# Inverse roots and small scalings as operations of their own in a fused attention and two-MoE kernel

## The chip, the cores and the metric

The kernel runs on one core of a Trainium2 chip. The metric is device time in microseconds (us) of one execution; the number that stands for a kernel is the median of its runs.

## The reference, cut to what matters

```python
def _attn_ref(q, k, v, g_q, g_k):            # batch 4, 12 heads, 448 tokens, 64 channels
    def rmsnorm(x, g):
        rms = np.sqrt(np.mean(x * x, axis=-1, keepdims=True) + 1e-06)
        return x / rms * g
    scores = np.matmul(rmsnorm(q, g_q), rmsnorm(k, g_k).transpose(0, 1, 3, 2)) / np.sqrt(64)
    scores = scores - np.max(scores, axis=-1, keepdims=True)
    attn = np.exp(scores)
    attn = attn / (np.sum(attn, axis=-1, keepdims=True) + 1e-09)
    return np.matmul(attn, v)

h = x @ w_in                                  # x is 1792 x 768, w_in 768 x 2048
g = h * (1.0 / (1.0 + np.exp(-1.702 * h)))    # first layer
x = g @ w_out                                 # w_out 2048 x 768
h = x @ w_in2                                 # second layer, same sizes
out = (h * np.clip(h + 3.0, 0.0, 6.0) / 6.0) @ w_out2
```

Attention, a first MLP layer and a second one follow each other. The weights of both layers arrive as 64-bit floats and are decoded on the chip.

## The kernel before

Every product of fp32 accuracy is made from two fp16 pieces (a high and a low one), so each layer matmul is three fp16 matmuls. The work is cut into four batches of 448 tokens. A batch goes through these stages:

- **Norm.** `sums_of` loads two heads of q and k, squares them (ACT or GpSimd) and sums the squares (VectorE, L974). `root` turns 14 or 28 columns of sums into inverse roots: nine small VectorE instructions, L1003 to L1018. `put` multiplies (L1028), splits into pieces (L1034, L1046, L1049) and transposes by DMA.
- **Units** (`add_units`), 24 groups of one or two tiles of 128 queries a batch. A group is: scores on PE into one of two `s` buffers (L1203, L1206), the row maximum on VectorE (L1211), a scaling of the maximum on ACT (L1215), the exponentials with their sums on ACT (L1216), which free the `s` buffer, a scaling of the sums on ACT (L1221), a reciprocal on VectorE (L1224). In batch 0 the probabilities are then turned by PE with a diagonal that holds 1/sum (L1265) and copied out (L1275 on ACT, L1276 on VectorE). In batches 1 to 3 they are split into pieces and turned by DMA. A product with v (L1164, in batch 0 L1131) ends each pair of heads; its result is split by ACT (L1297) and VectorE (L1302) into `xt`.
- **First layer.** `add_in1` is 16 blocks of 18 matmuls (L1410), each followed by a gate on ACT (L1455) and a product and a split on VectorE (L1459, L494). `add_out1` is 6 blocks of 48 matmuls (L1478), each followed by an evacuation on ACT (L1494). Beside the first layer of batch b stands the attention of batch b + 1. The first layer of batch b + 1 begins when the last out-block of batch b is on its way.
- **Second layer** (L1654 and L1769), over two halves of the tokens, after all batches.

Beside batch 0 the first weight W1 is decoded, beside batch 1 the second, W2 (L613, L617, L634, L494 and others).

What runs where and in which order is decided while the program is built. Each operation is entered with the engines that may take it and a cost in ns for each (`ways`), and a list scheduler (`Plan.order`) places all of them, by rank and by numbers in `CFG`: `own` and `off` shift the rank of single operations or of whole stages, `bias` charges an engine for an operation that others may take. The five engines then execute their queues strictly in order; an instruction that waits holds up all behind it on its engine. Where the plan leaves PE without work for some time it inserts filler matmuls (L1959).

## Time and profile before

| | |
|---|---|
| median of 3 runs | 1146.96 us (1146.66 to 1147.59) |
| the profiled execution | 1147.63 us |
| its span, first to last instruction | 1145.8 us |
| PE, VectorE, ACT, GpSimd busy | 1065.3, 822.5, 721.3, 365.1 us |
| mean granted clock of PE | 0.985 of full speed |

A share of busy time is a mean over stages with different limits. Which engine bounds a stage is read from the busy times of that stage and from what PE waits for in it.

### The profile page before, as it was taken

The numbers are of one execution on the slowest core, as the hardware profiler recorded it, in microseconds if no ns is written. First come the engines' busy times: TensorE is split into PE (matmuls) and PEld (weight loads), VectorE is DVE, ScalarE is ACT, GpSimd is POOL, SyncE is SP. The second block draws the span as 40 slices with busy tenths as digits, with TensorE's granted clock in tenths as the row PEclk, the third lists the DMA queues.
The fourth block names the chain that finished last, engine by engine and source line by source line (L and its number), as shares of the span: only waits on it lengthen the run. The fifth ranks groups of instructions, "written<-read, shape, count | busy, mean of one in ns | idle before, by whom it ended". The sixth has DMA issues, their size and how long they took to land. (4 is left out here: it accounts for less than half of the span.)

```text
span 1145.8 us, 18018 instructions
## 1 busy us (share of the span) xinstructions
PE 1065.3 (93%) x6571; PEld 588.7 (51%) x6571; DVE 822.5 (72%) x1445; ACT 721.3 (63%) x1505; POOL 365.1 (32%) x335
## 2 busy tenths in 40 slices
PE   3888964999999999999999999999999999999998
PEld 1566531554554555545555555555555555555555
DVE  7998889998699764797756878594577455935342
ACT  5999758999868996578885646463565132512210
POOL 6764555353156201350001255552132103200000
PEclk9999985999999999999999999999999999999999
DMA  8977578999976997569895327633451151222033
GB/s 239 193 199 192 167 203 212 204 191 222 241 227 187 173 176 155 181 194 166 171 185 154 120 78 264 231 108 120 146 189 55 56 169 40 71 72 98 1 90 104
DMA packets 236712, 178.88 MB, mean 156 GB/s; under 512 B 194896, under 2 KB 220496, under 8 KB 235088
## 3 DMA queue, kind: packets, MB, share of 16 engines
q1 hardware_dynamic: 236624, 177.74, 59.4%
q8 instruction: 51, 0.84, 0.3%
q14 instruction: 37, 0.30, 0.1%
HBM read 97.88 MB, written 34.41 MB: 115 GB/s over the span
## 5 line engine op out<-in xcount | busy, mean ns | idle before, releaser
L1410 PE MATMUL mm<-xt,wa 128*128 128x448 f16 x1152 | 229.5, 357 | 7.0 <-DVE st L1459 6.8
L1478 PE MATMUL mm<-gt,wb 128*128 128x448 f16 x1152 | 226.7, 352 | 0.7 <-DVE wb L494 0.5
L1769 PEld LDWEIGHTS <-gt 128*128 128x128 f16 x1344 | 131.4, 98 | 92.3 <-issue 4.8
L1410 PEld LDWEIGHTS <-wa 128*128 128x128 f16 x1152 | 113.9, 100 | 114.3 <-issue 14.5
L1478 PEld LDWEIGHTS <-wb 128*128 128x128 f16 x1152 | 111.8, 99 | 103.9 <-issue 1.1
L1654 PEld LDWEIGHTS <-xt 128*128 128x128 f16 x1008 | 98.6, 98 | 93.7 <-issue 3.8
L1216 ACT ACTIVATE p<-s,smalls 128x448 f32<-128x448 f32 x168 | 120.7, 720 | 7.5 <-DVE p L494 3.4
L1654 PE MATMUL s<-wa,xt 128*128 128x448 f16 x576 | 114.1, 352 | 2.1 <-DVE st L1669 2.1
L1211 DVE TENSOR_REDUCE smalls<-s 128x2 f32<-128x896 f32 (+1 forms) x96 | 91.5, 963 | 4.1 <-PE s L1206 3.9
L494 DVE SCALAR_TENSOR_TENSOR p<-p,smalls 128x448 f16<-128x448 f32 x108 | 78.1, 752 | 22.4 <-ACT p L479 22.1
L1203 PE MATMUL s<-gt 128*128 128x448 f16 (+1 forms) x192 | 62.2, 370 | 30.2 <-ACT p L1216 28.3
L1654 PE MATMUL mm<-wa,xt 128*128 128x448 f16 x432 | 86.9, 352 | 0.9 <-ACT wb L1676 0.9
L479 ACT ACTIVATE p<-p,smalls 128x448 f16<-128x448 f32 (+2 forms) x120 | 75.8, 666 | 11.7 <-DMA xt<-p 8.6
L1769 PE MATMUL mm<-p,gt 128*128 128x384 f16 x384 | 72.0, 326 | 0.0
L1769 PE MATMUL mm<-gt 128*128 128x384 f16 x372 | 68.2, 326 | 0.0
L1206 PE MATMUL s<-gt 128*128 128x448 f16 (+1 forms) x192 | 61.9, 366 | 0.0
L1769 PE MATMUL s<-p,gt 128*128 128x384 f16 x288 | 56.1, 326 | 2.4 <-ACT wb L1805 1.2
L1769 PE MATMUL s<-gt 128*128 128x384 f16 x300 | 55.9, 326 | 1.0 <-DVE st L1669 0.6
L494 DVE SCALAR_TENSOR_TENSOR gt<-st,smalls,gt 128x448 f16<-128x448 f32 x64 | 52.4, 829 | 6.1 <-ACT gt L479 4.9
L1808 DVE SCALAR_TENSOR_TENSOR wb<-mm,smalls,wb 128x384 f32<-128x384 f32 x47 | 27.0, 611 | 41.0 <-PE mm L1769 41.0
L479 ACT ACTIVATE gt<-st,smalls 128x448 f16<-128x448 f32 x49 | 32.1, 661 | 29.9 <-DVE st L1459 26.2
L1265 PE MATMUL mm<-gt,p 128*128 128x128 f32 x336 | 44.1, 280 | 6.3 <-DVE xt L1276 1.9
(216 smaller groups left out, 1827.4 us busy)
## 6 DMA issues: line engine op xcount, KB each, us to landing
wr<-in_moe_w_in_dram SPq DMA_DIRECT2D x32, 768.0 KB, 4.9
wa<-park_x SPq DMA_DIRECT2D x21, 672.0 KB, 4.0
wr<-in_moe_w_out_dram SPq DMA_DIRECT2D x12, 1024.0 KB, 6.4
wr<-in_moe_w_out_dram SPq DMA_DIRECT2D x16, 768.0 KB, 4.7
qkd<-xt SPq DMA_DIRECT2D x18, 672.0 KB, 4.7
p<-in_v_dram SPq DMA_DIRECT2D x42, 224.0 KB, 4.1
x2d<-st SPq DMA_DIRECT2D x24, 224.0 KB, 3.1
park_x<-wa SPq DMA_DIRECT2D x2, 2688.0 KB, 13.0
```

Of the source, the lines that this page charges most:

```text
L479: nc.scalar.activation(out=dst(), in_=src(), func=AF.Copy, scale=s)
L494: nc.vector.scalar_tensor_tensor(out=dst(), in0=src(), scalar=s, in1=high(), op0=ALU.mult, op1=ALU.subtract)
L1203: nc.tensor.matmul(o, lhsT=x[:, 64 * t:64 * t + m], rhs=x[:, 448:896], start=True, stop=False)
L1206: nc.tensor.matmul(o, lhsT=x[:, 64 * t:64 * t + m], rhs=x[:, 896:1344], start=False, stop=True)
L1211: nc.vector.tensor_reduce(out=nb, in_=s_t[sl.slot][:, :m, :S], axis=AX.X, op=ALU.max)
L1216: nc.scalar.activation(out=p(i), in_=s_t[sl.slot][:, i, :S], func=AF.Exp, bias=nb[:, i:i + 1], scale=alpha, accum_out=z[:, i:i + 1],)
L1265: nc.tensor.matmul(mm_t[tl.slot][:, 128 * j:128 * j + 128], lhsT=p(i)[:, c:c + 128], rhs=diag(), start=True, stop=True,)
L1410: nc.tensor.matmul(mm_t[ml.slot][:, :n], lhsT=w.inw(we, kc, f), rhs=x[:, xe, kc, :n], start=(kc == k0 and i == 0), stop=(kc == k1 - 1 and ...
L1478: nc.tensor.matmul(mm_t[ml.slot][:, :S], lhsT=W2.outw(we, fc, d * 128, 128), rhs=gv[:, ge_, fc, :], start=(fc == g.part.start and i == 0), ...
L1654: nc.tensor.matmul(self.bank(k), lhsT=w[:, we, fa, kc], rhs=xs[:, fb, xe, kc], start=first and kc == 0 and j == 0, stop=kc == 2 and j == 2 ...
L1769: nc.tensor.matmul(mm_t[banks[h].slot][:, :half], lhsT=g[:, ge, f, tb * 128:tb * 128 + 128], rhs=w4_t[part % 2][:, f, we, h * half:h * hal ...
L1808: nc.vector.scalar_tensor_tensor(out=view(), in0=bank(), scalar=self.co, in1=view(), op0=ALU.mult, op1=ALU.add)
```

## The change

Three pieces of code change, and the numbers that set the order.

1. The inverse root may run on GpSimd as well, as twelve instructions instead of nine (GpSimd is given two-operand steps).
2. The scaling of the maxima (before: the first instruction of a group's first exponential, ACT alone) and of the sums (before: the last instruction of the last exponential, ACT alone) become operations that ACT, GpSimd or VectorE may take.
3. `CFG` has other values throughout; the order of the whole program is planned anew from them.

```diff
-    bias=[2580, 340, 2500, 1380, 5660],
+    bias=[280, 520, 2440, 2180, 2580],
...
+        def root_pool(n, m):
+            o = 14 * (n % 4)
+            x, y, t, u = (r[:, o:o + 14 * m] for r in (msq, rsq, tsq, usq))
+            f = 0.375
+            pool, mul = nc.gpsimd.tensor_scalar, lambda a, b, c: nc.gpsimd.tensor_tensor(out=a, in0=b, in1=c, op=ALU.mult)
+            pool(out=x, in0=x, scalar1=2.0 ** -28, scalar2=1e-6 * 2.0 ** -22, op0=ALU.mult, op1=ALU.add)
+            pool(
+                out=y.bitcast(I32), in0=x.bitcast(I32), scalar1=-0.5, scalar2=float(0x5F3759DF),
+                op0=ALU.mult, op1=ALU.add,
+            )
+            mul(t, y, y)
+            mul(t, t, x)
+            pool(out=t, in0=t, scalar1=-0.5 * f, scalar2=1.5 * f, op0=ALU.mult, op1=ALU.add)
+            mul(y, y, t)
+            mul(t, y, y)
+            mul(t, t, x)
+            pool(out=u, in0=t, scalar1=1.0 / f ** 4, scalar2=-10.0 / 3.0 / (f * f), op0=ALU.mult, op1=ALU.add)
+            mul(t, t, u)
+            pool(out=t, in0=t, scalar1=5.0, scalar2=1.0, op0=ALU.add, op1=ALU.mult)
+            mul(y, y, t)
...
-                (DVE, 2300, lambda n=grp[0], m=m: root(n, m)), sum((p[1] for p in parts), [])
+                [(DVE, 2300, lambda n=grp[0], m=m: root(n, m)), (POOL, 2900, lambda n=grp[0], m=m: root_pool(n, m))],
+                sum((p[1] for p in parts), []),
...
-                    if i == 0:
-                        nc.scalar.activation(out=nb, in_=nb, func=AF.Copy, scale=nalpha)
...
-                    if i == m - 1:
-                        nc.scalar.activation(out=z, in_=z, func=AF.Copy, scale=2.0 ** -14, bias=1e-9 * 2.0 ** -14)
...
+                o = op([
+                    (ACT, 200, lambda nb=nb, late=late: nc.scalar.activation(
+                        out=nb, in_=nb, func=AF.Copy, scale=nalpha, bias=UP if late else 0.0)),
+                    (POOL, 300, lambda nb=nb, late=late: nc.gpsimd.tensor_scalar(
+                        out=nb, in0=nb, scalar1=nalpha, scalar2=UP if late else 0.0, op0=ALU.mult, op1=ALU.add)),
+                    (DVE, 130, lambda nb=nb, late=late: nc.vector.tensor_scalar(
+                        out=nb, in0=nb, scalar1=nalpha, scalar2=UP if late else 0.0, op0=ALU.mult, op1=ALU.add)),
+                ], [o])
...
+                    o = op([
+                        (ACT, 200, lambda z=z: nc.scalar.activation(
+                            out=z, in_=z, func=AF.Copy, scale=2.0 ** -14, bias=1e-9 * 2.0 ** -14)),
+                        (POOL, 300, lambda z=z: nc.gpsimd.tensor_scalar(
+                            out=z, in0=z, scalar1=2.0 ** -14, scalar2=1e-9 * 2.0 ** -14, op0=ALU.mult, op1=ALU.add)),
+                        (DVE, 130, lambda z=z: nc.vector.tensor_scalar(
+                            out=z, in0=z, scalar1=2.0 ** -14, scalar2=1e-9 * 2.0 ** -14, op0=ALU.mult, op1=ALU.add)),
+                    ], es)
```

The diff also carries a second way of dividing by the sums (`late`) and a parameter for which head pairs take batch 0's way of turning (`plain`). With the values given (`defer` all zero, `plain` six pairs of batch 0 and none after it) the first is never used and the second leaves each batch as it was. One small memset is added at the start.

Counted in the whole program: ten of the eleven 28-column roots go to GpSimd (one of them in batch 0, three in each later batch), and the two 14-column roots of batch 0 stay on VectorE. Of the 96 scalings of maxima 20 go to GpSimd and one to VectorE, of the 96 of sums 31 and two; in batch 0 it is 20 and 20 on GpSimd, in batch 1 none. The matmuls are the same ones, with 47 fillers for 36. Much else that may run on several engines changes hands with the new plan, most of it from GpSimd to VectorE: a subtraction of low pieces of probabilities (L509 on GpSimd, L510 on VectorE) 11 times, splits of q (L1046) 12 times.

Three places of the order follow. In them the lines of the new kernel are higher by some 8 to 90: L1069, L1087, L1090, L1256, L1548, L502, L487, L1583, L1358 and L1602 are L1028, L1046, L1049, L1211, L1459, L494, L479, L1494, L1297 and L1513 of before.

GpSimd, from the end of batch 0 (the product that ends the splitting of W1) into the norm of batch 1, before (L977 multiplies k by the gains, `xt` holds q and k):

```order
L509 TENSOR_TENSOR wa<-wb,wa 128x6x128
L977 TENSOR_TENSOR xt<-xt,gp 128x448 x2
L1028 TENSOR_TENSOR xt<-xt,smalls 128x448 x2
L1049 TENSOR_TENSOR xt<-xt 128x7x64
L1046 TENSOR_TENSOR xt<-xt 128x7x64
L485 TENSOR_SCALAR gt<-st,smalls 128x448
```

And of the change:

```order
L996 TENSOR_TENSOR xt<-xt,gp 128x448 x2
L1045 TENSOR_SCALAR smalls<-smalls 128x28
L1046 TENSOR_SCALAR smalls<-smalls 128x28
L1044 TENSOR_TENSOR smalls<-smalls 128x28 x2
L1052 TENSOR_SCALAR smalls<-smalls 128x28
L1044 TENSOR_TENSOR smalls<-smalls 128x28 x3
L1056 TENSOR_SCALAR smalls<-smalls 128x28
L1044 TENSOR_TENSOR smalls<-smalls 128x28
L1058 TENSOR_SCALAR smalls<-smalls 128x28
L1044 TENSOR_TENSOR smalls<-smalls 128x28
L1069 TENSOR_TENSOR xt<-xt,smalls 128x448 x2
```

The twelve instructions of batch 1's first root now stand on GpSimd between the gains and the products with the roots.

VectorE, up to the first two maxima of batch 1 (`s_75` and `s_76` are the two score buffers), before:

```order
L1018 SCALAR_TENSOR_TENSOR smalls<-smalls 128x28
L628 TENSOR_SCALAR wr<-wr 128x1024
L1028 TENSOR_TENSOR xt<-xt,smalls 128x448 x2
L634 SCALAR_TENSOR_TENSOR wr<-wr 128x1024
L1049 TENSOR_TENSOR xt<-xt 128x7x64 x2
L1211 TENSOR_REDUCE smalls<-s_75 128x2
L1211 TENSOR_REDUCE smalls<-s_76 128x2
```

And of the change:

```order
L653 SCALAR_TENSOR_TENSOR wr<-wr 128x1024
L1548 SCALAR_TENSOR_TENSOR st<-st,mm_73 128x448
L502 SCALAR_TENSOR_TENSOR gt<-st,smalls,gt 128x448 x2
L1069 TENSOR_TENSOR xt<-xt,smalls 128x448 x2
L1090 TENSOR_TENSOR xt<-xt 128x7x64 x2
L1256 TENSOR_REDUCE smalls<-s_75 128x2
L1087 TENSOR_TENSOR xt<-xt 128x7x64
L1548 SCALAR_TENSOR_TENSOR st<-st,mm_72 128x448
L1548 SCALAR_TENSOR_TENSOR st<-st,mm_71 128x448
L1256 TENSOR_REDUCE smalls<-s_76 128x2
```

The root is gone from VectorE there, and more products and splits of the first layer of batch 0 (L1548, L502) stand ahead of and between the maxima.

ACT, where batch 1's attention ends (L1297 is the last split of a product with v, L1494 the evacuation of an out-block of batch 0), before:

```order
L479 ACTIVATE wb<-wr 128x16x64
L1297 ACTIVATE xt<-mm_72 128x448
L1308 ACTIVATE p,smalls<-xt 128x448
L1494 ACTIVATE st<-mm_74,smalls 128x448
L1513 ACTIVATE mm_74,smalls<-st 128x448
L925 ACTIVATE p,smalls<-p 128x448 x5
L971 ACTIVATE p<-xt 128x448 x2
L925 ACTIVATE p,smalls<-p 128x448
L971 ACTIVATE p<-xt 128x448 x2
L1494 ACTIVATE st<-mm_73,smalls 128x448
```

And of the change:

```order
L487 ACTIVATE wb<-wr 128x16x64
L487 ACTIVATE p<-p,smalls 128x448
L1583 ACTIVATE st<-mm_74,smalls 128x448
L487 ACTIVATE gt<-p,smalls 128x7x64
L1602 ACTIVATE mm_71,smalls<-st 128x448
L1602 ACTIVATE mm_74,smalls<-st 128x448
L487 ACTIVATE gt<-p,smalls 128x7x64
L808 ACTIVATE wr<-wr 128x768
L1358 ACTIVATE xt<-mm_72 128x448
L1369 ACTIVATE p,smalls<-xt 128x448
```

Before, two out-blocks were still to be evacuated behind the last split; now one is. On PE, 51 out-matmuls of batch 0 stood behind the last product of batch 1, now 21 do; and 17 of the fillers stand ahead of the last 27 out-matmuls that precede that product.

## Rows read from the trace of the kernel before

**Rows 1.** The page, busy time of each engine in us, its share and count

```profile
PE 1065.3 (93%) x6571; PEld 588.7 (51%) x6571; DVE 822.5 (72%) x1445; ACT 721.3 (63%) x1505; POOL 365.1 (32%) x335
```

**Rows 2.** The table of stretches: busy us (and count) of each engine in each

```profile
core 0: us, PE busy (x) PEld busy (x) DVE busy (x) ACT busy (x) POOL busy (x), PEclk, DMA share, GB/s
28.60:107.00 78.40, 69.24 (x501) 46.97 (x500) 73.93 (x132) 75.62 (x194) 50.38 (x56) 1.00 0.79 192
134.20:168.80 34.60, 25.02 (x128) 12.50 (x126) 28.42 (x60) 21.82 (x36) 19.79 (x15) 0.95 0.76 215
168.80:220.00 51.20, 34.27 (x189) 16.60 (x190) 50.12 (x84) 43.89 (x100) 27.11 (x22) 0.73 0.89 217
220.00:305.80 85.80, 81.10 (x605) 44.54 (x603) 71.66 (x137) 80.88 (x178) 30.66 (x26) 1.00 0.93 208
305.80:316.00 10.20, 10.04 (x56) 5.30 (x57) 5.93 (x21) 7.73 (x22) 1.74 (x2) 1.00 0.85 268
316.00:1145.80 829.80, 811.19 (x4887) 441.36 (x4885) 548.76 (x926) 453.58 (x895) 201.93 (x174) 1.00 0.51 137
```

**Rows 3.** The waits of PE, 134 to 220 us: total, times, longest

```profile
PE s L1203 <- ACT p L1216: 14.7, 4, 4.9
PE mm L1410 <- DVE st L1459: 6.5, 2, 5.8
```

**Rows 4.** Groups of instructions, ACT: busy us, mean ns of one

```profile
L1215 ACT ACTIVATE smalls<-smalls 128x2 f32<-128x2 f32 (+1 forms) x96 | 27.3, 284 | 8.8 <-DVE smalls L1211 8.7
L1221 ACT ACTIVATE smalls<-smalls 128x2 f32<-128x2 f32 (+1 forms) x96 | 19.5, 203 | 3.1
L1275 ACT COPY xt<-mm 128x512 f32<-128x512 f32 x17 | 9.7, 572 | 1.1 <-PE mm L1265 1.1
L479 ACT ACTIVATE wa<-wb,smalls 128x768 f16<-128x768 f32 (+2 forms) x14 | 12.4, 916 | 0.0
```

**Rows 5.** Timeline of GpSimd: one diagonal by itself

```profile
106.22 0.37 POOL L485 TENSOR_SCALAR gt<-gt,smalls 128x128 f32<-128x128 f32 x1 [0.52 <-PE mm L1265]
```

**Rows 6.** Groups of instructions, GpSimd: busy us, mean ns of one

```profile
L485 POOL TENSOR_SCALAR gt<-gt,smalls 128x128 f32<-128x128 f32 x28 | 17.4, 626 | 22.5 <-DVE smalls L1224 16.7 <-PE mm L1265 4.8 <-ACT wa L479 0.6
L1028 POOL TENSOR_TENSOR xt<-xt,smalls 128x448 f32<-128x448 f32 x21 | 22.6, 1098 | 17.1 <-DVE smalls L1018 14.7 <-DVE smalls L932 2.0 <-DVE smalls L459 0.4
```

**Rows 7.** Timeline of VectorE: first and last of nine root instructions

```profile
142.84 0.17 DVE L1003 TENSOR_SCALAR smalls<-smalls 128x28 f32<-128x28 f32 x1
...
144.60 0.19 DVE L1018 SCALAR_TENSOR_TENSOR smalls<-smalls 128x28 f32<-128x28 f32 x1
```

**Rows 8.** Timelines of PE and VectorE at batch 1's first scores

```profile
163.39 0.35 PE L1203 MATMUL s<-gt 128*128 128x448 f16 x1
...
168.75 2.07 DVE L1211 TENSOR_REDUCE smalls<-s 128x2 f32<-128x896 f32 x2
```

**Rows 9.** Groups of instructions, VectorE

```profile
L494 DVE SCALAR_TENSOR_TENSOR gt<-st,smalls,gt 128x448 f16<-128x448 f32 x64 | 52.4, 829 | 6.1 <-ACT gt L479 4.9 <-POOL gt L485 0.9
L1459 DVE SCALAR_TENSOR_TENSOR st<-st,mm 128x448 f32<-128x448 f32 x64 | 38.6, 610 | 4.7 <-ACT st L1455 4.6
L1028 DVE TENSOR_TENSOR xt<-xt,smalls 128x448 f32<-128x448 f32 x15 | 17.2, 1176 | 0.0
L1276 DVE COPY xt<-mm 128x512 f32<-128x512 f32 x25 | 16.8, 679 | 0.3 <-PE mm L1265 0.2
L510 DVE TENSOR_TENSOR p<-p 128x448 f16<-128x448 f32 x1 | 1.4, 1449 | 0.0
```

**Rows 10.** Groups of instructions, ACT, of work beside batch 1

```profile
L479 ACT ACTIVATE wb<-wr,smalls 128x1024 f16<-128x1024 f32 x7 | 8.0, 1136 | 1.1 <-DVE smalls L468 1.1
L1455 ACT ACTIVATE st<-mm,smalls 128x448 f32<-128x448 f32 x64 | 39.1, 619 | 8.0 <-PE mm L1410 7.4 <-DVE gt L494 0.3 <-DVE smalls L459 0.3
L1494 ACT ACTIVATE st<-mm,smalls 128x448 f32<-128x448 f32 x24 | 14.9, 620 | 15.1 <-PE mm L1478 15.1
```

**Rows 11.** Timeline of PE behind batch 1's last product

```profile
308.46 7.54 PE L1478 MATMUL mm<-gt,wb 128*128 128x448 f16 x39
```

More of the change, by code (lines that the diff above doesn't have):

```diff
@@ L524, in constants @@
         nc.gpsimd.memset(one, 1.0)
+        nc.gpsimd.memset(ones, 1.0)
         make_identity(nc, ident)
@@ L1147, in add_pair @@
             loads.append(sp(
-                128 * m * 256, load, loads[:1] or [bt.vscale] + batches[0].pvs, takes=None if loads else raw_l, wide=False
+                128 * m * 256, load, loads[:1] or [bt.vscale] + batches[0].pvs + after, takes=None if loads else raw_l, wide=False
             ))
@@ L1335, in add_units @@
-                if early:
-                    def put(n=n, both=both):
-                        queue().dma_start(
-                            out=xd[b % 2][n], in_=both().rearrange("p e c -> p (e c)")
-                        )
-                    def get(n=n):
-                        queue().dma_start(
-                            out=xt[:, :, n, :], in_=xd[b % 2][n].rearrange("p (e c) -> p e c", e=2)
-                        )
-                    early.left = 2
-                    sq.also.append(early)
-                    x = sp(128 * 1792, put, [x], gives=early)
-                    x = sp(128 * 1792, get, [x] + x_after, wide=False)
@@ L1350, in add_units @@
-                bt.xlow.append(x)
+                    if zl:
+                        for r in range(max(len(x) for x in runs)):
+                            for i in range(7):
+                                for h in range(2):
+                                    if r < len(runs[h]):
+                                        c, q0, m, s, w = runs[h][r]
+                                        nc.tensor.matmul(
+                                            mm_t[zl.slot][64 * h:64 * h + 64, c:c + m * w], lhsT=ones,
+                                            rhs=pt[:, s:s + w, i, q0:q0 + m], start=i == 0, stop=i == 6,
+                                        )
@@ L1351, in add_units, with each_head @@
+                o = op(
+                    (PE, (19 if late else 12) * t_pe(S) + 700, both_heads), deps[0] + deps[1] + vdone,
+                    takes=[ml, zl] if late else ml, gives=vl,
+                )
+                pv_done = o
+                if late:
+                    o = op((ACT, t_act(S), offset), [o], takes=ql, gives=zl)
+                    o = op((DVE, 2 * t_dve(S) + 60, divide), [o], gives=ql)
             else:
-                ml = Lease(mm_ring)
                 products, deps, vls = zip(*ready)
-                def both(ml=ml, products=products):
+                def each_head(ml=ml, products=products):
@@ L1359, in both, with put, get @@
                                 product_(ml, i, j)
[L1361 removed]
+                o = pv_done = op((PE, 2400, each_head), deps[0] + deps[1], takes=ml, gives=vls[0])
                 o.also = [vls[1]]
[L1363 to L1366 removed]
+            pv = [pv_done, pv_done]
+            h = op((ACT, t_act(S, int(plain)), bind(xhigh, ml, slice(0, 128))), [o] + ([bt.vscale] if plain else []) + x_free, takes=early)
+            x = op((DVE, t_dve(S) + 30, bind(xlow, ml, slice(0, 128))), [h], gives=ml)
+            sq = op((ACT, t_act(S, 1), xsquare), [h], takes=bl, gives=bl)
+            xmax.append(sq)
+            if early:
+                def put(n=n, both=both):
+                    queue().dma_start(
+                        out=xd[b % 2][n], in_=both().rearrange("p e c -> p (e c)")
+                    )
+                def get(n=n):
+                    queue().dma_start(
+                        out=xt[:, :, n, :], in_=xd[b % 2][n].rearrange("p (e c) -> p e c", e=2)
+                    )
+                early.left = 2
+                sq.also.append(early)
+                x = sp(128 * 1792, put, [x], gives=early)
+                x = sp(128 * 1792, get, [x] + x_after, wide=False)
+            bt.xlow.append(x)
             for i in range(7):
```

112 lines of the change are left out of this document (65 added, 47 removed), and 24 rows, old and new, of the table own.

## Prediction

> **What bounds the kernel now.** I read the page first, then what PE waited for, then the busy times of all engines stretch by stretch. PE is busy 1065.3 of the span's 1145.8 us [rows 1], so some 80 us are open to any change of order, and the question is where they lie. From 316 us on PE is busy 811.19 of 829.80 us [rows 2]: PE is the bound there, and no order can take more than 18.6 us out of three quarters of the span. The other 62 us lie ahead of 316 us, in the norm and attention of batches 0 and 1, where the first layer is not there yet, or only batch 0's.
>
> There the reader is to see which engine is full. From 28.6 to 107 us, in batch 0, ACT is busy 75.62 and VectorE 73.93 of 78.40 us, PE 69.24 [rows 2]: ACT is the bound, VectorE close behind it. From 168.8 us, where the first maximum of batch 1 begins, to 220 us VectorE is busy 50.12 of 51.20 us, PE 34.27 at 0.73 of its clock; from 220 to 305.8 us, where batch 1's last product is done, ACT is busy 80.88 of 85.80 us [rows 2]. PE's waits agree: between 134 and 220 us it waits 14.7 us for exponentials to free a score buffer and 6.5 us for the product that frees an accumulator [rows 3]. So up to 305.8 us the time is set by the queues of ACT and VectorE. A change there counts by what it adds to these two, and by how much PE has left to do once batch 1's attention is over: 10.20 us of PE work stand between that and the first layer of batch 1 at 316 us [rows 2].
>
> The profiled execution took 1147.63 us, 1.83 more than its span, and 0.67 more than the median of the three runs shown. The sum is made against 1147.63. About 0.2%, 2.3 us, is what a measurement of this kernel can tell from no change.
>
> **The change part by part.** Counts are from the order of instructions before and after, durations from the rows (busy time over count).
>
> *Batch 0, scalings and one root.* ACT loses 21 scalings of maxima at 0.284 us and 22 of sums at 0.203 us, -10.4 us [rows 4]. The new plan gives most of it back: 11 more copies of turned tiles at 0.57 (+6.3) and 4 more halves of W1 at 0.89 (+3.5) [rows 4]; of other kinds two fewer, some -1. ACT: about -1.7 us. VectorE loses the 11 copies at 0.67 and a root of 1.95 us, and takes nine two-input pieces of 448 columns at up to 1.15 from GpSimd [rows 9, 7]: even. The price is the way through GpSimd. No scaling of one or two columns is in its trace; the nearest rows are the diagonals of 128 columns, 0.37 us by itself and 0.626 on the mean beside other work [rows 5, 6]. A maximum thus takes 0.09 to 0.34 us longer than on ACT, and 20 of them 1.7 to 6.9 us if each lies on the path. ACT, with 2.8 us of idle time in 78 [rows 2], mostly has other work in its queue meanwhile, so I take 0.7. Batch 0: **-1 us**, ends -1.7 and +5.2.
>
> *Batch 1's first root.* On VectorE nine instructions took 1.95 us, from 142.84 to 144.79 [rows 7]. Twelve on GpSimd at 0.37 to 0.626 take 4.4 to 7.5 us, 2.5 to 5.6 longer, and behind them stand the products with the roots, the splits, the store, the transposes and the first scores. What covers it is VectorE's own lateness: the first scores began on PE at 163.39 us, but their maximum at 168.75 [rows 8], because VectorE had a second root, decoding and norm pieces ahead of it. A chain that comes 5 us later meets a queue that is not shorter (the change puts three more gate splits there for the two roots it takes out). If that cover were gone it would cost its whole 2.5 to 5.6. I take **0**, ends 0 and +5.6. The roots of batches 2 and 3 lie beside a first layer that keeps PE full; there I take nothing.
>
> *Batch 1's attention, 137.0 us from 168.8 to 305.8.* ACT's work in it was 124.8 us, VectorE's 121.8 [rows 2]. ACT loses three splits of W2 at 1.14 and three gates at 0.61, and gains two gate splits and five single instructions of 0.55 to 0.9 [rows 10]: even, within 0.5 us. VectorE loses a root (1.95), three gate splits at 0.82 and a product at 0.60, but takes from GpSimd seven subtractions of low probabilities and three norm pieces, at 1.15 to 1.45 each [rows 7, 9], and a microsecond of decoding: +8 us, to 129.8. VectorE becomes the longer queue. How full it can be is seen in the rows: ACT was 91% busy over this stretch, 94% in its second part, 96% in batch 0 [rows 2]. At 91% 129.8 us of work take 142.6 us, at 94% 138, at 96% 135. I take 139, near the middle value: **+2 us**, ends -2 and +5.6.
>
> *The tail behind it.* Before, 51 out-matmuls of batch 0 stood behind batch 1's last product; now 21 do. Thirty at 0.193 (39 take 7.54 [rows 11]) are **-5.7 us**. It is real only if PE has done the thirty by then. It can: at the first product of batch 1 PE now stands 81 matmuls further on in the first layer, 282 for 201, which is where the 14.7 us of waits for exponentials were; 81 at 0.193 are 15.6 us, the thirty need 5.7. The 17 fillers ahead of the last out-block show that the plan has PE idle there.
>
> *From 316 us on.* VectorE takes over further pieces from GpSimd, 15 combinations in the second layer among them. It is busy 548.76 of 829.80 us there [rows 2], so 281 us of idle time cover it, and PE has the same matmuls: **0**, ends -3 and +3. The other fillers number 30 for 36 and fall into planned idle time; the memset at the start lies ahead of the first input. Nothing.
>
> At one place the Trainium skill speaks against the change. The rows have the product of 448 columns with the roots on both engines, 1.098 us on GpSimd and 1.15 on VectorE [rows 6, 9]: for this form GpSimd is no slower here. The Trainium skill's "GPSIMD Engine Reference", section "Engine selection", says to keep elementwise products on VectorE, since GpSimd is about twice as slow with two inputs; by the row a root of twelve steps at VectorE's 0.22 each takes 2.6 us and the sum stays, by the rule seven of them take 0.43, the root 4.1, and the sum rises by up to 2.2 us where nothing covers it. The trace does not agree for the wide form, and shows no narrow one.
>
> **Sum.** -1 + 0 + 2 - 5.7 + 0 = -4.7 us, against 1147.63: 1142.9. As a median, somewhat under the profiled execution, **1142.5 us**.
>
> **Rivals.**
>
> *GpSimd's queue sets batch 0's pace* (slower). GpSimd executes in order, and a scaling of a maximum stands behind diagonals, W1's decoding and norm pieces. If each of the 20 waits for one diagonal (0.626) and takes as long itself, against 0.284 on ACT, that is 0.97 each, 19 us, of which ACT's other work hides perhaps half: +10 in place of +0.7, so 1152. For it: GpSimd was busy 50.38 of 78.40 us there already [rows 2]. Against it: ACT's queue is long. From 0.24 us a maximum on (4.7 over 20) no gain is left.
>
> *VectorE at its old density in batch 1* (slower). At 91% the stretch takes 5.6 us more; with the root's 2.5 uncovered it is -1 + 2.5 + 5.6 - 5.7 = +1.4, 1149. For it: 168.8 to 220 us is already full. Beyond +6.7 for root and stretch together it decides.
>
> *The roots on GpSimd start every attention late* (slower). The upper price of the chain, 5.6 us, in the open once, in batch 1, makes -4.7 + 5.6: 1148.5. Against it: the 5.4 us of lateness on VectorE. By the rule of the page above this is the case to expect, since a root would then be slower on GpSimd at any width.
>
> *The change moves waits without shortening them* (the same). PE waits at the end of batch 1 for what it did not wait for at 170 us, and the tail's 5.7 us come back as a later last product: 1147. For it: the fillers there; VectorE's sum grows.
>
> *A denser batch 1* (faster still). GpSimd holds fewer wide two-input instructions, and VectorE runs as densely as ACT in batch 0: 135 for 137, root covered, -1.7 in batch 0, and 3 us of PE's 18.6 idle after 316: -1.7 - 2 - 5.7 - 3 = -12.4, 1135.
>
> **How the numbers follow.** Forecast (1139 to 1146) 0.42; GpSimd in batch 0 0.16; density 0.12; late roots 0.06; waits moved 0.13; denser 0.11. Faster by over 0.2% are the denser case and nearly all of the forecast, 0.51; slower are the first rival, most of the density case and half of the late roots, with the upper ends of others, 0.29; the rest, 0.20, is the same. The range goes from 1134, the denser case's value and a little, to 1153, the first rival's and a little.
>
> **What would show it.** Right: in batch 0 ACT's busy share stays at 96% or more and no wait of ACT for GpSimd's scalings is among the long ones; between 134 and 220 us PE's waits for exponentials fall from 14.7 to under 5; the last product of batch 1 is done between 303 and 310 us and batch 1's first layer begins 4.5 us behind it; behind that PE is as full as before. Wrong: batch 0's attention ending later than 136 us with ACT waiting for GpSimd; a first maximum of batch 1 well behind 169 us; or a last product of batch 1 behind 312 us, which takes back the whole tail.

## The result, and the profile after

The changed kernel takes 1161.20 us (median of 4 runs, 1158.25 to 1163.10) against 1146.81 for the kernel before beside it (1144.26 to 1147.59): a ratio of 1.0127, 95% interval 1.0097 to 1.0157. It is slower by 14.4 us, outside the predicted range. The profiled execution took 1159.57 us with a span of 1157.8, 12.0 longer than before's; the places below are found in that pair.

The engines as a whole hardly tell it. The page's busy row, against [rows 1]:

```profile
PE 1071.5 (93%) x6582; PEld 591.9 (51%) x6582; DVE 813.3 (70%) x1402; ACT 731.4 (63%) x1485; POOL 334.2 (29%) x429
```

VectorE (DVE) has 9 us less work and the kernel is slower, so the loss is not in VectorE's work. Where it grows is seen by the start of the same instruction in both traces (us from the span's start):

| place | before | after | later by |
|---|---|---|---|
| batch 0, sixth product scaled | 133.5 | 137.2 | 3.7 |
| batch 1, first maximum | 168.8 | 172.2 | 3.4 |
| batch 1, sixth product scaled | 305.8 | 315.3 | 9.5 |
| batch 0, last out-matmul of the first layer | 315.6 | 318.1 | 2.5 |
| batch 1, last in-matmul | 381.8 | 385.4 | 3.6 |
| batch 2, last in-matmul | 526.6 | 538.2 | 11.6 |
| second layer, first matmul | 721.8 | 731.3 | 9.5 |
| last instruction | 1145.5 | 1157.5 | 12.0 |

Up to 318 us the plan costs 2.5 us; 7.0 come between there and the second layer, and 2.5 in the second layer. The table of stretches for these two parts, columns as in [rows 2], first of the kernel before and then of the changed one:

```profile
315.80:721.80 406.00, 398.29 (x2514) 209.29 (x2513) 303.67 (x541) 296.61 (x658) 123.94 (x111) 1.00 0.72 176
721.80:1145.80 424.00, 413.09 (x2376) 232.26 (x2374) 245.25 (x386) 156.97 (x237) 78.19 (x63) 1.00 0.31 100
```

```profile
28.60:107.00 78.40, 65.80 (x471) 44.73 (x471) 68.06 (x123) 69.37 (x162) 53.88 (x82) 0.96 0.78 199
...
318.30:731.30 413.00, 400.37 (x2513) 210.74 (x2512) 298.62 (x521) 305.87 (x669) 104.60 (x154) 0.98 0.72 173
731.30:1157.80 426.50, 413.81 (x2375) 231.84 (x2373) 248.60 (x399) 164.91 (x245) 60.34 (x48) 1.00 0.32 99
```

PE does the same 2513 matmuls in 413.0 us that it did in 406.0. It idles 12.6 us there in place of 7.7, and its granted clock has fallen to 0.98: of the 7.0 us, 4.9 are idle time and 2.1 longer busy time. The stretch of 28.6 to 107 us answers the first of [rows 2]: ACT, busy 75.62 us before, is busy 69.37.

The roots are next. The timeline of the second root of batch 2 on GpSimd (first and last of twelve instructions), and what VectorE and PE did around it:

```profile
345.37 0.61 POOL L1045 TENSOR_SCALAR smalls<-smalls 128x28 f32<-128x28 f32 x1 [2.33 <-DVE smalls L993]
...
349.21 0.25 POOL L1044 TENSOR_TENSOR smalls<-smalls 128x28 f32<-128x28 f32 x1
349.53 2.65 POOL L1069 TENSOR_TENSOR xt<-xt,smalls 128x448 f32<-128x448 f32 x2
```

```profile
345.82 0.61 DVE L1548 SCALAR_TENSOR_TENSOR st<-st,mm 128x448 f32<-128x448 f32 x1
349.49 1.91 DVE L1069 TENSOR_TENSOR xt<-xt,smalls 128x448 f32<-128x448 f32 x2 [3.05 <-POOL smalls L1044]
```

```profile
347.64 0.56 PE L1248 MATMUL s<-gt 128*128 128x448 f16 x1 [3.49 <-DMA gt<-qkd]
```

The root takes 4.09 us, from 345.37 to 349.46; before, the nine instructions of [rows 7] took 1.95. Behind it stand the four normalisations (the products with the roots, L1069) of two pairs of heads, two on each engine; they begin together. VectorE, from which the root was taken, stands idle for 3.05 of those 4.09 us, because the next instruction in its queue is one of the four. PE meanwhile waits 3.49 us for the transposed q and k of the pairs ahead, which came through the first root. VectorE's wait repeats in every root of batches 1 to 3, as the waits of VectorE from 137 to 735 us say (total, times, longest):

```profile
DVE xt L1069 <- POOL smalls L1044: 17.0, 9, 3.1
```

Nine roots at 1.95 would be 17.5 us of VectorE's time; it waits 17.0 for the nine. Hardly any of VectorE's time was freed. The mean of the nine roots is 4.39 us, against 2.37 before (some were slowed by other work).

Batch 3 shows what a wait costs PE. Its timeline, and the table of stretches:

```profile
518.18 0.53 PE L1248 MATMUL s<-gt 128*128 128x448 f16 x1 [1.35 <-ACT p L1259]
...
523.98 5.62 PE L1499 MATMUL mm<-xt,wa 128*128 128x448 f16 x18 [3.77 <-DVE st L1548]
```

```profile
514.00:518.00 4.00, 1.46 (x7) 0.58 (x6) 2.28 (x3) 2.98 (x10) 3.50 (x8) 0.99 1.11 240
518.00:528.00 10.00, 6.05 (x16) 2.27 (x16) 9.64 (x17) 9.84 (x24) 2.92 (x3) 0.50 0.51 166
528.00:532.00 4.00, 4.00 (x22) 2.10 (x21) 2.90 (x8) 3.27 (x9) 0.00 (x0) 0.98 1.17 220
```

PE was busy 1.46 of 4 us, then ran at 0.50 of its clock, the lower of its two levels (1.2 GHz), for 10 us, and was back behind that. A wait thus costs more than its own length. The wait of 3.77 us for a gate product is not due to the roots: with all of them back on VectorE it is 4.7 us long (below).

The scalings, against [rows 4]: groups on GpSimd (and, last, the root's products), and ACT's wait for them in batch 0 (25 to 137 us), which did not exist before:

```profile
L1280 POOL TENSOR_SCALAR smalls<-smalls 128x2 f32<-128x2 f32 (+1 forms) x20 | 13.2, 661 | 6.7 <-DVE smalls L1256 3.9 <-DVE smalls L1297 1.4 <-DVE smalls L1265 1.2
L1295 POOL TENSOR_SCALAR smalls<-smalls 128x2 f32<-128x2 f32 (+1 forms) x31 | 9.3, 301 | 132.2 <-ACT p L1259 129.1 <-DMA p<-in_v_dram 2.7
L1044 POOL TENSOR_TENSOR smalls<-smalls 128x28 f32<-128x28 f32 x70 | 19.8, 283 | 5.7
```

```profile
ACT p L1259 <- POOL smalls L1280: 6.7, 6, 2.7
```

And PE's waits from 137 to 220 us, against [rows 3]: those for exponentials fell from 14.7 to 3.7 us, as predicted, but those for gate products rose from 6.5 to 13.5.

```profile
PE mm L1499 <- DVE st L1548: 13.5, 3, 7.2
PE s L1248 <- ACT p L1259: 3.7, 3, 1.9
```

### The profile page after: what moved, and what is told of

It is laid out like the page before. It is cut to its first block, busy times and chain, and to the rows that moved or that the text cites. A ratio compares the mean times of both kernels' runs of the same rounds, so it can differ in the third digit from the quotient of the medians.

```text
span 1157.8 us, 18015 instructions
## 1 busy us (share of the span) xinstructions
PE 1071.5 (93%) x6582; PEld 591.9 (51%) x6582; DVE 813.3 (70%) x1402; ACT 731.4 (63%) x1485; POOL 334.2 (29%) x429
## 4 chain that ended last, share of the span: by engine, by line
PE 64%; ACT 10%; DVE 9%; DMA 6%; POOL 5%; issue 4%; SPq 2%; POOLq 0%; ACTq 0%; DVEq 0%
PE mm L1567 14%; PE s L1858 9%; PE mm L1858 9%; PE s L1743 8%; PE mm L1499 8%; PE mm L1743 7%; PE mm L1206 3%; ACT p L1259 3%; PE mm L1173 2%; PE s L1248 2%; POOL smalls L1044 1%; DMA xt<-p 1%; PE s L1251 1%; PE mm L1326 1%; ACT p L487 1%
## 5 line engine op out<-in xcount | busy, mean ns | idle before, releaser
L1499 PE MATMUL mm<-xt,wa 128*128 128x448 f16 x1152 | 232.1, 361 | 17.3 <-DVE st L1548 17.3
L1567 PE MATMUL mm<-gt,wb 128*128 128x448 f16 x1152 | 229.2, 355 | 1.6 <-DVE wb L518 0.8
L1743 PE MATMUL s<-wa,xt 128*128 128x448 f16 x531 | 105.7, 352 | 0.8 <-DVE st L1758 0.8
L1256 DVE TENSOR_REDUCE smalls<-s 128x2 f32<-128x896 f32 (+1 forms) x96 | 92.4, 965 | 10.9 <-PE s L1251 10.6
L502 DVE SCALAR_TENSOR_TENSOR p<-p,smalls 128x448 f16<-128x448 f32 x108 | 77.4, 745 | 30.3 <-ACT p L487 30.1
L1743 PE MATMUL mm<-wa,xt 128*128 128x448 f16 x477 | 96.6, 352 | 0.6 <-ACT wb L1765 0.6
L487 ACT ACTIVATE p<-p,smalls 128x448 f16<-128x448 f32 (+2 forms) x128 | 81.8, 672 | 8.9 <-DMA xt<-p 7.2
L1858 PE MATMUL s<-gt 128*128 128x384 f16 x360 | 75.4, 326 | 2.5 <-DVE wb L1897 1.9
L1858 PE MATMUL s<-p,gt 128*128 128x384 f16 x312 | 64.5, 326 | 3.6 <-ACT wb L1894 1.2
L1897 DVE SCALAR_TENSOR_TENSOR wb<-s,smalls,wb 128x384 f32<-128x384 f32 x44 | 25.8, 612 | 45.0 <-PE s L1858 45.0
L502 DVE SCALAR_TENSOR_TENSOR gt<-st,smalls,gt 128x448 f16<-128x448 f32 x64 | 48.1, 760 | 6.0 <-ACT gt L487 5.4
L1544 ACT ACTIVATE st<-mm,smalls 128x448 f32<-128x448 f32 x64 | 39.5, 622 | 14.6 <-PE mm L1499 13.2
```

The costliest lines, as they stand in the source:

```text
L487: nc.scalar.activation(out=dst(), in_=src(), func=AF.Copy, scale=s)
L502: nc.vector.scalar_tensor_tensor(out=dst(), in0=src(), scalar=s, in1=high(), op0=ALU.mult, op1=ALU.subtract)
L1256: nc.vector.tensor_reduce(out=nb, in_=s_t[sl.slot][:, :m, :S], axis=AX.X, op=ALU.max)
L1499: nc.tensor.matmul(mm_t[ml.slot][:, :n], lhsT=w.inw(we, kc, f), rhs=x[:, xe, kc, :n], start=(kc == k0 and i == 0), stop=(kc == k1 - 1 and ...
L1544: nc.scalar.activation(out=t, in_=m, func=AF.Tanh, scale=bt.c1[:, f:f + 1])
L1567: nc.tensor.matmul(mm_t[ml.slot][:, :S], lhsT=W2.outw(we, fc, d * 128, 128), rhs=gv[:, ge_, fc, :], start=(fc == g.part.start and i == 0), ...
```

## The experiments

Three theories: **late roots** (the chain behind a root is on the path), **slow scalings** (ACT waits for them), **the order itself** (the plan of all other work). Most kernels keep one order row for row and only issue chosen operations to another engine, after the planner is done. In the diffs `o.ways[0][1]` is an operation's planned cost: 2300 for a root, 200 for a scaling.

### Engines exchanged under a kept order

```diff
         for o in self.done:
+            if o.way[0] == POOL and o.ways[0][1] == 2300:    # first and third run
+                o.way = o.ways[0]                             # root to VectorE
+            if o.way[0] == POOL and o.ways[0][1] == 200:     # second and third run
+                o.way = o.ways[0]                             # scaling to ScalarE
             o.way[2]()
```

**All roots back.** 

> The changed kernel with its order kept row for row, but all ten inverse roots that GpSimd takes issued to VectorE at the same places of the order. Late roots (a root takes 4 to 5 us on GpSimd against 2 to 2.9 on VectorE, and each batch's attention starts behind it): 1149 to 1154 us, with the first transposes of q and k of batches 1 and 2 some 2 us earlier. Slow scalings on GpSimd: no change, 1159 to 1163. The order itself: no change either, 1158 to 1163, since the order stays.

Measured: 1152.04 us, 1.0056 of before (1.0034 to 1.0077): 9.2 less than the changed kernel, as late roots expected. The waits of PE from 318 to 735 us, first of the changed kernel, then of this run:

```profile
PE s L1248 <- ACT p L1259: 5.1, 4, 2.0
PE mm L1499 <- DVE st L1548: 3.8, 1, 3.8
PE s L1248 <- DMA gt<-qkd: 3.5, 1, 3.5
```

```profile
PE mm L1501 <- DVE st L1550: 4.7, 1, 4.7
PE s L1250 <- DMA gt<-qkd: 1.3, 1, 1.3
PE s L1250 <- ACT p L1261: 1.1, 3, 0.6
```

The waits for exponentials and for q and k fall from 8.6 to 2.4 us; the one for a gate product stays, so it belongs to the order. A second price of the moved root shows behind it. With the root on VectorE the two engines' normalisations run one pair after the other (the first root of batch 2, GpSimd and VectorE):

```profile
329.57 1.83 POOL L1071 TENSOR_TENSOR xt<-xt,smalls 128x448 f32<-128x448 f32 x2 [2.48 <-issue]
331.47 1.14 DVE L1071 TENSOR_TENSOR xt<-xt,smalls 128x448 f32<-128x448 f32 x2
```

Behind a root on GpSimd they begin together and take 2.65 and 1.91 us, as shown above. The lengths of all 36 of batches 1 to 3 add up to 33.5 us in this run and to 42.2 in the changed kernel.

**All scalings back.** 

> The changed kernel with its order kept, but every scaling of maxima and sums that GpSimd takes issued to ScalarE at the same place of the order. Slow scalings: 1152 to 1157 us, ScalarE's 6.7 us of waits for scaled maxima in batch 0 gone. Late roots: no change, 1159 to 1163. The order itself: 1158 to 1163, batch 0's attention still ends near 137.

Measured: 1163.94 us, 1.0154 (1.0130 to 1.0178). ACT's wait is gone, and nothing is won: batch 0's sixth product is scaled at 138.7 in place of 137.2. GpSimd's scalings help this order a little, so slow scalings is ruled out for it.

**Both.** 

> The changed kernel's order with roots on VectorE and scalings on ScalarE, so that only the order and the choice of engines for the other operations differ from the kernel before. Late roots or slow scalings, or both: 1146 to 1151 us. The order itself: 1157 to 1163, no better than the changed kernel.

Measured: 1155.61 us, 1.0085 (1.0060 to 1.0109). That lies between the two expected ranges: the order with the choice of the other engines costs 8.5 us of its own beside before's 1147.14, and the scalings on GpSimd give 3.6 of them back (1155.61 to 1152.04).

The reverse, in the order of the kernel before:

```diff
-                (DVE, 2300, lambda n=grp[0], m=m: root(n, m)), sum((p[1] for p in parts), [])
+                (DVE, 2300, lambda n=grp[0], m=m: (root_pool if (b, grp[0]) in ROOTS else root)(n, m)),
+                sum((p[1] for p in parts), []),
```

**Before, with roots on GpSimd.** 

> The kernel before with its order kept row for row, but the same ten roots (batch 0's first, and all of batches 1 to 3) issued to GpSimd at their places. Late roots: 1152 to 1160 us. Slow scalings or the order itself: 1146 to 1149, as the kernel before.

As run, batch 0's root stayed on VectorE and the nine of batches 1 to 3 moved. Measured: 1164.63 us, 1.0164 (1.0135 to 1.0192), above the range of late roots: 17.5 us for nine roots, more than their own lengthening of 14.1 (9 times 3.94 less 2.37). PE's waits of that run from 318 to 740 us have one of 6.4 us:

```profile
PE s L1227 <- ACT p L1240: 8.2, 3, 6.4
```

**Before, with scalings moved.** The same by a list of the order of before, with the changed kernel's engines for the scalings alone. 

> The order of the kernel before, with its roots on VectorE, and each scaling of a maximum or a sum as an instruction of its own on the engine that the changed kernel's plan gives it (53 on GpSimd, a few on VectorE, the rest on ScalarE). Scalings on GpSimd are the half of the change that pays (putting them back cost the changed order 3 us): 1143 to 1146. They make ScalarE wait in an order that was not made for them: 1148 to 1153.

As run, 51 scalings are on GpSimd. Measured: 1157.15 us, 1.0084 (1.0067 to 1.0102), above both expectations. In batch 0 ACT waits, and the sixth product is scaled at 145.0 in place of 133.5; of these 11.5 us 9.0 are left at the end of the span. What the new plan does for the scalings is to hide this:

```profile
ACT p L1327 <- POOL smalls L1348: 18.0, 14, 2.8
```

### How long a root may be

**Only first roots back.**

```diff
+            if o.way[0] == POOL and o.ways[0][1] == 2300 and o.key in (918, 1674, 2424):
+                o.way = o.ways[0]
```

> The changed kernel's order, with only the first of the three roots of batches 1, 2 and 3 issued to VectorE and the other two left on GpSimd. Roots in series (each of a batch's three roots lengthens the chain that brings its q and k by its own 2 us): a third of the 9 us that all three gave, 1157 to 1159. Only the start counts (the first root decides when an attention begins): nearly all of it, 1151 to 1154.

Measured: 1161.23 us, 1.0124 (1.0100 to 1.0148): nothing won, less even than a third. The start of an attention is not what counts; why a third of the roots gives nothing is seen in the table of chains below.

**GpSimd's formula on VectorE.**

```diff
+        def root_long(n, m):    # root_pool's twelve steps, nc.vector for nc.gpsimd
...
+                o.way = (DVE, 2300, o.long)    # for roots on GpSimd
```

> The changed kernel's order, with the ten roots on VectorE in GpSimd's formula of twelve instructions in place of VectorE's own nine. The engine makes a root long: about 2.6 us a root and 1152 to 1155, near the run with nine instructions. The three more instructions make it long: 4 us a root and 1159 to 1162.

Measured: 1163.23 us, 1.0137 (1.0118 to 1.0156), with roots of 2.59 us. That fits neither: the roots are as short as the first theory said, and the time is that of the second. The Trainium skill's "VectorE: DVE Perf Modes", section "Rules for kernel authors", says to keep the count of operations in a chain small; this run agrees: twelve instructions took 2.59 us where nine took 1.94. 0.65 us more a root cost 11 us, so I took other lengths, on VectorE and in the changed order, and a short one in the order of before:

```diff
+        def root_short(n, m):   # the first five of root's nine instructions
+        def root_twice(n, m):   # root, then ten more in a row through usq into y
+        def root_six(n, m):     # one third-order step: y *= 1.875 - 1.25 s + 0.375 s * s, s = x * y * y
```

**Five instructions.** 

> The changed kernel's order, with its ten GpSimd roots on VectorE and only the first refinement of each (five instructions in place of nine; the second refinement is left out). About 1.1 us a root in place of 1.95. The chain of roots bounds (twelve instructions on VectorE, 0.65 us more a root, took 11 us more): some 5 to 11 us less than with nine, 1141 to 1148. The roots already fit with nine instructions and only longer ones show: 1150 to 1153.

Measured: 1146.11 us, 0.9986 (0.9975 to 0.9998), in the range of the first theory: the roots bound this order.

**Nineteen.** 

> The changed kernel's order, with its ten GpSimd roots on VectorE and each made as long as on GpSimd (nine instructions and ten more that change nothing, about 4.1 us). The length of a root counts, whichever engine has it: 1161 to 1167, at or a little above the changed kernel, since VectorE is also held for it. The loss grows without bound with the length on VectorE: 1168 to 1180.

Measured: 1178.20 us, 1.0270 (1.0251 to 1.0289), in the range of the second theory. These roots are 4.18 us long, no longer than the changed kernel's on GpSimd, and the time is 17.0 us above it. So the engine counts beside the length: a root on VectorE costs more than an equally long one on GpSimd.

**Five, in the kernel before.** 

> The kernel before with its order, and roots of batches 1 to 3 cut to their first refinement (five instructions in place of nine, the second refinement left out). The chain of roots bounds this kernel too (nine roots longer by 2 us each took 17.5 us more): 9 roots x 0.85 us shorter, 1137 to 1143. It bounds only once roots get longer: 1146 to 1148.

Measured: 1141.89 us, 0.9955 (0.9937 to 0.9974). The chain bounds the old order too.

**Six, in the kernel before.** 

> The kernel before with its order, and roots of batches 1 to 3 in six instructions: one third-order refinement in place of a second-order and a third-order one (a coarser root, by the formula about 1e-4 of its value). About 1.3 us a root in place of 1.95. The chain of roots and VectorE bound this kernel (five instructions took 4.9 us off): 1141 to 1144. Only the shortest root shows: 1146 to 1147.

Measured: 1143.69 us, 0.9969 (0.9955 to 0.9984). With a coarser root, these two are faster than both kernels.

### What is held, or what is late

**VectorE held, nothing waiting.** The ten more instructions write only a scratch column. 

> The changed kernel's order, with its ten GpSimd roots on VectorE in nine instructions, and ten more instructions behind each root that hold VectorE as long as in the run with 4.1 us roots, but on whose result nothing waits. Only the chain counts (sums, root, normalisation): 1151 to 1155, as with nine instructions. VectorE's time counts as much as the chain: 1163 to 1168, about half of the 26 us that the 4.1 us roots took. Only VectorE's time counts: 1175 to 1180, as with the 4.1 us roots.

Measured: 1183.33 us, 1.0312 (1.0287 to 1.0337), above all three expectations. The timeline of VectorE at batch 2's first root, which ends at 339.55:

```profile
339.46 3.48 DVE L1069 SCALAR_TENSOR_TENSOR smalls<-smalls 128x28 f32<-128x28 f32 x10
...
344.22 1.15 DVE L1081 TENSOR_TENSOR xt<-xt,smalls 128x448 f32<-128x448 f32 x2
```

VectorE's two normalisations (L1081) begin 4.7 us behind the root, 2.0 us behind it in the run with all roots back (331.47 behind 329.43): what stands in VectorE's queue there delays them as a longer root does. The ten took 3.48 us here, where the ten of the run with nineteen took 2.2 (4.18 less 1.94), because two of them ran beside GpSimd's normalisations (last section). VectorE was thus held longer than in that run, which the expectations had not allowed for.

**VectorE's normalisations to GpSimd.**

```diff
+            if (o.way[0] == DVE and o.ways[0][0] == POOL and len(o.ways) == 2
+                    and any(d.ways[0][1] == 2300 and d.way[0] == POOL for d in o.deps)):
+                o.way = o.ways[0]
```

> The changed kernel's order with its roots on GpSimd, but those normalisations behind a GpSimd root that stand in VectorE's queue (two of a root's four, the first of which waited for the root each time, 17.0 us over nine roots) issued to GpSimd too. VectorE's wait in its own queue is what the moved root costs: that wait gone, 1150 to 1156. The chain behind the root is what it costs, and it gets longer still (four normalisations one after the other): 1160 to 1166.

Measured: 1164.50 us, 1.0162 (1.0138 to 1.0186). The 17.0 us of waits are gone and come back one step further down the chain, longer, at the next instruction that VectorE has in it:

```profile
DVE xt L1093 <- ACT xt L1078: 29.1, 9, 5.0
```

So that idle time of VectorE is not the price by itself; the chain behind the root is, which here has the four normalisations one after the other. Its length can be read: from the start of a batch's first root to the end of its third, since a pair's q and k are loaded over those of the pair two before it, once that is normalised and split. Sum over batches 1 to 3, from the traces:

| kernel | mean root, us | three chains, us | time, us |
|---|---|---|---|
| before, five instructions | 1.38 | 92.4 | 1141.9 |
| before, six | 1.71 | 95.5 | 1143.7 |
| before | 2.37 | 101.7 | 1146.8 |
| before, roots on GpSimd | 3.94 | 116.4 | 1164.6 |
| new order, five | 1.06 | 100.0 | 1146.1 |
| new order, nine | 1.94 | 106.1 | 1152.0 |
| new order, twelve on VectorE | 2.59 | 113.2 | 1163.2 |
| new order, first roots back | 3.65 | 119.2 | 1161.2 |
| changed kernel | 4.39 | 121.2 | 1161.2 |
| new order, normalisations to GpSimd | 4.40 | 122.1 | 1164.5 |
| new order, nine and VectorE held | 1.95 | 122.9 | 1183.3 |
| new order, nineteen on VectorE | 4.18 | 125.5 | 1178.2 |

The chains are those of one profiled execution each, and the times are medians. In the old order 24.0 us of chain are 22.7 us of time, unevenly: from 92.4 to 101.7 us 9.3 are worth 4.9, from there to 116.4 us 14.7 cost 17.5. In the new order 25.5 us are 32.1, but not evenly either: three first roots back shorten the chain by only 2.0 us, and between 113 and 121 us the time does not rise. The kernels from 119 to 122 us have roots on GpSimd, the one at 113 has all on VectorE, and the two that hold VectorE longest lie far above the rest. So the chain alone does not give the time: a longer root on VectorE lengthens the chain and holds VectorE as well, and how the two share the price stays open.

### The order by parts

The order was written out as a list: that of before up to a place, behind it all that is left in the changed kernel's (or the reverse), roots of batches 1 to 3 on VectorE.

```diff
-        for _ in self.ops:
-            best = None
...
+        for code in struct.unpack('<%dH' % (len(raw) // 2), raw):
+            o, e = by[code // 8], code % 8
```

**Batch 0 of before.** 

> The order of the kernel before until batch 0's sixth and last product is scaled, then all that is left in the changed kernel's order, with roots of batches 1 to 3 on VectorE (scalings of batch 0 are then ScalarE's again). The order of batch 0 costs: the last product at 133 to 134 in place of 138.7 and, if that lead stays, 1146 to 1149. The lead is lost again behind it: 1151 to 1154, as with all roots on VectorE.

**The rest of before.** 

> The changed kernel's order, roots of batches 1 to 3 on VectorE, until batch 0's first layer has done its last product (319.1 with all roots on VectorE), then all that is left in the order of the kernel before. The order behind 319 costs nothing of its own once the roots are back: 1150 to 1153. It costs the 2.5 us that the second layer showed: 1148 to 1150.

**Second layer of after.** 

> The order of the kernel before until the second layer's first product, then the changed kernel's order. The new order of the second layer costs its 2.5 us by itself: 1148.5 to 1150, with 426 us from the second layer's first product to the end. Those 2.5 us came from what ran ahead of it (lateness carried in): 1146 to 1147.5, 424 us.

Measured: 1153.40, 1154.78 and 1156.61 us (1.0053, 1.0076, 1.0072). All three are inconclusive: each took the filler matmuls of the skipped part along to its seam, where the two lists meet, 20, 30 and 42 of them, 9 us of PE's time in the third. Two were run again without (20 is right where the expectation has 18):

**Batch 0 again.** 

> Again the order of the kernel before until batch 0's last product is scaled and the changed kernel's behind it with roots of batches 1 to 3 on VectorE, without the 18 filler matmuls that the run before carried to the seam (3.9 us there, partly in TensorE's idle time). The order of batch 0 costs and the lead stays: 1146 to 1150. The lead is lost behind it: 1151 to 1153.5, as with all roots on VectorE.

Measured: 1151.97 us, 1.0055 (1.0035 to 1.0075), the time of the run with all roots back. The sixth product is scaled at 133.5, a lead of 5.2 us, of which 2.3 are left at the second layer in the profiled pair and none in the medians.

**Second layer again.** 

> Again the order of the kernel before until the second layer's first product and the changed kernel's behind it, without the 42 filler matmuls that the run before carried to the seam (9 us of TensorE work there). The new order of the second layer costs its 2.5 us by itself: 1148 to 1150.5. Carried in: 1146 to 1147.5.

Measured: 1147.67 us, 1.0013 (1.0000 to 1.0027). It lies between the two expected ranges, and by the times alone the cost is 0 to 3.1 us. By the profile its second layer takes the same 426.50 us as the changed kernel's, and before's takes 424.00:

```profile
722.40:1148.90 426.50, 413.85 (x2376) 231.89 (x2373) 248.27 (x399) 164.87 (x245) 60.61 (x48) 1.00 0.31 99
```

All thirteen traces with that order there, and no fillers carried to it, have 426.5 us, whether it begins at 715.7 or at 754.7 us; the six with the order of before have 424.0 to 426.0. So the new order of the second layer costs 0.5 to 2.5 us by itself, and nothing was carried in. Single spans divide the 12.0 us into 6.3 for the roots (1157.8 to 1151.5), 2.3 for batch 0's order (to 1149.2), 2.5 for the second layer and 0.9 for the rest, but executions of one kernel lie several us apart (6.4 in the run of batch 0 again). By the medians the roots are 9.2 of 14.4 us, batch 0's order is nothing, the second layer 0 to 3.1, and 2 to 5 us are not located.

## Why the prediction was wrong

The terms were -1 + 0 + 2 - 5.7 + 0. In the same parts the spans differ by 3.7 - 0.3 + 6.1 - 7.0 + 7.0 + 2.5 = 12.0 us.

**From 316 us on: 0, measured 7.0 and 2.5.** This is the step that failed: "The roots of batches 2 and 3 lie beside a first layer that keeps PE full; there I take nothing." PE's 811.19 of 829.80 us [rows 2] were read as cover. But PE is full there only as long as scores come in time; with the roots back on VectorE the stretch to the second layer takes 405.7 us again (406.0 before, 413.0 after). In two other runs of this order with nine instructions on VectorE it takes 407.7 (both back) and 408.9 (batch 0 again), so 4 to 7 of the 7.0 us go with the roots. Six roots were costed at nothing, where each lengthens a chain that the old order already paid for: five instructions in place of nine made the kernel before faster by 4.9 us. Of the second layer, "281 us of idle time cover it" failed by 2.5 us, just inside the end of +3.

**The late-roots rival** had the mechanism in part. A root takes 4.09 us against 1.95 undisturbed and delays what stands behind it, but it is not the start of an attention that costs, since first roots back won nothing. It was priced once, in batch 1, and given 0.06. The Trainium skill's "GPSIMD Engine Reference", section "Engine selection" (about twice as slow with two inputs), beside it had the right sign. What the prediction set against that rule, 1.098 us on GpSimd and 1.15 on VectorE for the wide product, was misread: both are means over products of which many ran beside the other engine. The trace of before has two by themselves on each engine, 0.94 us apiece on GpSimd and 0.62 on VectorE, 1.5 to one:

```profile
144.87 1.83 POOL L1028 TENSOR_TENSOR xt<-xt,smalls 128x448 f32<-128x448 f32 x2 [2.02 <-DVE smalls L1018]
147.73 1.15 DVE L1028 TENSOR_TENSOR xt<-xt,smalls 128x448 f32<-128x448 f32 x2
```

Length and engine both show: twelve instructions on VectorE (2.59 us) were no faster than the changed kernel, nineteen (4.18 us) 17.0 us slower.

**Batch 0: -1, measured +3.7.** The scaling of a maximum on GpSimd costs 0.661 against 0.284 us on the mean, 0.38 more and just beyond my upper 0.34, but in this order it pays a little (the run with scalings back is slower). The term was lost in the order: with that of before the sixth product comes at 133.5 again. ACT's busy share fell to 88%, where 96% was named as the sign of being right. The rival of GpSimd setting the pace is what the scalings did in the old order, at its predicted size (11.5 us against 10), but not in the new one.

**Batch 1's first root: 0, measured -0.3.** It took 4.16 us, under my 4.4 to 7.5. The first score on PE [rows 8] is 5.1 us later, of which batch 0 brings 3.7; the first maximum is 3.4 us later, less than batch 0 alone. The number held, but partly by luck. The cover was read from the old order, and there it fails: from batch 0's sixth product to that maximum are 35.3 us before, 37.5 with roots on GpSimd and 32.7 with five instructions. It is the new order that hides the root (35.0 us, 34.6 with the roots back).

**Batch 1's attention: +2, measured +6.1** (137.0 to 143.1 us), past its end of 5.6. With the roots back it is 142.5 and with five instructions 141.9, so it is the order. The chain of the three roots in batch 1 goes the same way, 34.9 us before, 40.9 with the roots back and 44.8 in the changed kernel, but its last 3.9 us hardly show in the stretch; what in the order does it stays open. The term's mechanism failed: VectorE was to have 129.8 us of work there and to be the longer queue. It was busy 121.1 of the 143.1 us and ACT 123.2, no more than before, so both were less dense (85% and 86%) and not fuller:

```profile
172.20:315.30 143.10, 122.91 (x827) 65.03 (x827) 121.11 (x213) 123.22 (x279) 51.95 (x51) 0.93 0.87 213
```

**The tail: -5.7, measured -7.0** (from the last product to the last out-matmul 9.8 before, 2.8 after). Right (thirty at 0.193 are 5.8), and eaten by the lateness ahead of it.

## What to carry to other kernels

A chain of short operations that gates the next stage is not covered by a busy matrix engine if the next stage's matmuls come out of it: measure the chain from its first link to its last in each repetition, and price a longer link at its added length times its repetitions before taking any cover. That is a first estimate only: for nine roots on GpSimd it gives 14.1 us in the old order, which cost 17.5, and 22.0 (9 times 4.39 less 1.94) in the new one, which cost 9.2. Taking an operation off a busy engine frees little if that engine's next instruction waits for the result; look at who stands next in its queue, and at what the two engines then begin together. A shorter, coarser formula on the same engine beat every placement tried here.

## What the runs showed of the hardware

An instruction of 28 columns takes 0.19 us on VectorE [rows 7] and 0.283 on the mean on GpSimd. The same twelve took 2.59 us on VectorE and 4.09 on GpSimd, so that of the root's factor of 2 about 1.6 is the engine and 1.33 the longer formula.

VectorE and GpSimd hold each other up. The ten extra instructions took 0.189 us each where GpSimd waited for them, and 0.300 on the mean where its normalisations ran beside them. That mean is of two kinds: 83 of the 100 took 0.18 to 0.19 us, and 17, beside a normalisation on GpSimd, 0.81 to 0.93. These are VectorE's group in the run with nineteen instructions, then in the run that held VectorE (first the mean, then shortest, median and longest in ns):

```profile
L1069 DVE SCALAR_TENSOR_TENSOR smalls<-smalls 128x28 f32<-128x28 f32 x90 | 17.0, 189 | 3.1
```

```profile
L1069 DVE SCALAR_TENSOR_TENSOR smalls<-smalls 128x28 f32<-128x28 f32 x100 | 30.0, 300 | 3.1
...
L1069 DVE SCALAR_TENSOR_TENSOR smalls<-smalls x100: 179/189/928, 27.4 to 537.8; 128x28 f32<-128x28 f32 x100
```

The normalisations do it to each other: 0.62 us by itself on VectorE and 0.94 on GpSimd, and up to 1.46 and 1.38 in batches 1 to 3 of the changed kernel, where both engines begin theirs together behind each root (shortest, median, longest):

```profile
L1069 DVE TENSOR_TENSOR xt<-xt,smalls x19: 624/1356/1455, 148.0 to 516.7; 128x448 f32<-128x448 f32 x19
L1069 POOL TENSOR_TENSOR xt<-xt,smalls x17: 1312/1375/1381, 148.0 to 517.6; 128x448 f32<-128x448 f32 x17
```

The Trainium skill's "GPSIMD Engine Reference", section "1. Specifications", states that GpSimd's SBUF interfaces are shared with VectorE, with contention where a VectorE instruction has two inputs from SBUF; these rows, of instructions with two such inputs, agree.
